# A shorter fallback path behind the last branch: four loops in place of six

## The chip, the core and the metric

The kernel runs on one core of one Trainium2 chip. The core has a matrix engine (PE, with PEld for its weight loads), a vector engine (DVE), a scalar engine (ACT), a general engine (POOL) and SP, which only issues transfers and waits. Each has its own stream of instructions, which is loaded from memory while it runs; in the profile these loads are packets of kind "instruction" (queue q8 for PE, q14 for the others). The metric is the device time of one execution in microseconds; the median of the runs counts.

## What is computed

Pooled attention, then a multiplicative feed-forward block. In the reference, cut to what matters:

```python
# q, k, v: (8, 8, 1152, 64); w1, w2: (512, 1024); w3: (1024, 1024); w_out: (1024, 512)
q_pool = q.reshape(B, H, S // 2, 2, D).mean(axis=3)          # 576 queries
scores = (1 / np.sqrt(D)) * np.matmul(q_pool, k.transpose(0, 1, 3, 2))
scores = scores - np.max(scores, axis=-1, keepdims=True)
attn = np.exp(scores)
attn = attn / (np.sum(attn, axis=-1, keepdims=True) + 1e-09)
x = np.matmul(attn, v)             # then (8 * 576, 512)
out = ((x @ w1) * (x @ w2)) @ w3 @ w_out
```

## The kernel before

The kernel has two paths that compute the same thing. The fast path is one long unrolled program: 32 pairs of heads, scores of 512 columns at a time (L450), exp without the maximum on ACT (L455), the product with the values (L481), and the feed-forward block in chunks of 512 rows filled in between (L590, L628), with w3 and w_out multiplied beforehand into T16. The order on PE is planned when the program is built (`_visits`).

Leaving the maximum out is sound only while the sums of the exponentials stay in a range. The fast path keeps the reciprocal of each sum in `rzall`; near the end DVE compares them with two bounds, a matmul counts how many are inside, and `badi` holds the number of those that aren't. `nc.values_load` reads it into a register of each engine (L1019). At L1022 stands the branch, `tc.If(bad > 0)`: each engine compares its register with zero; if nothing is bad, it jumps over the fallback path, `_general`, to the end of the program. With the inputs of the reference nothing is bad, so `_general` is never executed. It is there, in the instruction streams, between the branch and the end.

The last two chunks of rows (`late_chunks`, L684) run in an order written out by hand (`LATE_ORDER`), in a form with seven products in place of eight (L725), whose sums DVE takes (L776) and whose scaled copies ACT makes (L770, L792). Each finished quarter is stored (`stored`, L736; the transfer itself is L602). `LATE_BY_ACT` names six of these stores that ACT issues on its own transfer queue, q10, in place of SP (q1):

```python
eng = nc.scalar if f"o{k[1]}{k[2]}{c}" in LATE_BY_ACT else nc.sync
...
LATE_BY_ACT = "o00c21 o01c12 o10c12 o10c21 o11c12 o11c21".split()
```

The last of all, o01c12, is ACT's. At the target of the branch (booked under L1022) each engine waits for its own work to be done, and SP for the eight stores that may still be under way, one semaphore after the other; ACT's last four stores stand first, in the order in which they were issued. Behind it, under L1049, SP does twelve further waits that clear the semaphores, and all engines meet at a barrier, twice; there the span ends.

`_general` itself has the loops over batches (`ib`), pairs of heads (`ip`), steps of 96 queries (`iq`, once for each head of a pair, written out twice), tiles of the hidden width (`ift`), and steps of 96 rows for the last product (`iq` again): six in the program. Each loop brings, on every engine, blocks for its entry, its reset with barriers, its back branch and its exit. In the compiled program the instructions between the branch and its target number 261 on PE, 233 on SP, 221 on DVE, 160 on ACT and 156 on POOL, branch labels not counted.

Of the kernel before, what the change touches and what calls it, by code (L numbers as in the profile page):

```python
# [8 lines left out]
FP32 = mybir.dt.float32  # L9
FP16 = mybir.dt.float16  # L10
AF = mybir.ActivationFunctionType
ALU = mybir.AluOpType
# [11 lines left out]
def _general(tc, q, k, v, out, w1sb, w2sb, T16):  # L24

    nc = tc.nc
    B, H, S, D = q.shape
    Sq = S // 2
    NJ = S // 128
    dm = H * D  # L30
    dff = w1sb.shape[2]
    NC = dm // 128
    NF = dff // 128
    QP = 96
    QC = Sq // QP
    SCALE = 0.5 * float(D) ** -0.5
    SCL = 16.0
    W = 384
    kf, qf, vf = (t.rearrange("b h s d -> (b h) s d") for t in (k, q, v))
    with tc.tile_pool(name="gen", bufs=1) as sb, \  # L40
         tc.tile_pool(name="gen_ps", bufs=1, space=bass.MemoryType.PSUM) as ps, \
         tc.For_i(0, B, 1) as ib:
        xT = sb.tile([128, NC * Sq], FP16)
        with tc.For_i(0, H // 2, 1) as ip:
            for u in range(2):
                ih = ib * H + ip * 2 + u
                hs = u * 64
                kst = sb.tile([128, NJ, D], FP32, tag="g_kst")
                nc.sync.dma_start(out=kst, in_=kf[bass.ds(ih, 1)].rearrange("o (c p) d -> p (o c) d", p=128))
                vst = sb.tile([128, NJ, D], FP32, tag="g_vst")  # L50
                nc.sync.dma_start(out=vst, in_=vf[bass.ds(ih, 1)].rearrange("o (c p) d -> p (o c) d", p=128))
                qst = sb.tile([QP, QC, 2, D], FP32, tag="g_qst")
                nc.sync.dma_start(out=qst, in_=qf[bass.ds(ih, 1)].rearrange("o (c p t) d -> p (o c) t d", p=QP, t=2))
                kh = sb.tile([128, NJ, 128], FP16, tag="g_kh")
                qh = sb.tile([QP, QC, 128], FP16, tag="g_qh")
                vh = sb.tile([128, NJ, D], FP16, tag="g_vh")
                nc.vector.memset(kh, 0.0)
                nc.vector.memset(qh, 0.0)
                nc.vector.tensor_copy(out=kh[:, :, 0:D], in_=kst)
                nc.vector.tensor_tensor(out=qh[:, :, 0:D], in0=qst[:, :, 0, :], in1=qst[:, :, 1, :], op=ALU.add)  # L60
                nc.vector.tensor_copy(out=vh, in_=vst)
                kT = sb.tile([128, NJ, 128], FP16, tag="g_kT")
                nc.sync.dma_start(out=kT, in_=kh.rearrange("p c d -> p (c d)"), transpose=True)
                qT = sb.tile([128, QC * QP], FP16, tag="g_qT")
                nc.sync.dma_start(out=qT.rearrange("p (c i) -> p c i", i=QP), in_=qh.rearrange("p c d -> p (c d)"),
                                  transpose=True)
                kTf = kT.rearrange("p c i -> p (c i)")
                with tc.For_i(0, Sq, QP) as iq:
                    qc = sb.tile([128, QP], FP16, tag="g_qc")
                    nc.vector.tensor_copy(out=qc, in_=qT[:, bass.ds(iq, QP)])  # L70
                    pss = ps.tile([128, S // W, 512], FP32, tag="g_pss")
                    for w in range(S // W):
                        nc.tensor.matmul(pss[0:QP, w, 0:W], qc, kTf[:, w * W:w * W + W], start=True, stop=True)
                    mx = sb.tile([QP, 1], FP32, tag="g_mx")
                    nc.vector.tensor_reduce(out=mx, in_=pss[0:QP, :, 0:W], axis=mybir.AxisListType.XY, op=ALU.max)
                    nb = sb.tile([QP, 1], FP32, tag="g_nb")
                    nc.vector.tensor_scalar_mul(out=nb, in0=mx, scalar1=-SCALE)
                    e = sb.tile([QP, S // W, W], FP32, tag="g_e")
                    nc.scalar.activation(out=e, in_=pss[0:QP, :, 0:W], func=AF.Exp, bias=nb, scale=SCALE)
                    z = sb.tile([QP, 1], FP32, tag="g_z")  # L80
                    nc.vector.tensor_reduce(out=z, in_=e, axis=mybir.AxisListType.XY, op=ALU.add)
                    nc.vector.tensor_scalar(out=z, in0=z, scalar1=1e-9, scalar2=None, op0=ALU.add)
                    rz = sb.tile([QP, 1], FP32, tag="g_rz")
                    nc.vector.reciprocal(out=rz, in_=z)
                    eh = sb.tile([QP, S], FP16, tag="g_eh")
                    nc.vector.tensor_scalar(out=eh, in0=e.rearrange("p w i -> p (w i)"), scalar1=rz, scalar2=SCL,
                                            op0=ALU.mult, op1=ALU.mult)
                    eT = sb.tile([128, NJ, QP], FP16, tag="g_eT")
                    nc.sync.dma_start(out=eT, in_=eh, transpose=True)
                    pav = ps.tile([128, 512], FP32, tag="g_pav")  # L90
                    pc = pav[hs:hs + 64, 0:QP]
                    for jt in range(NJ):
                        nc.tensor.matmul(pc, vh[:, jt, :], eT[:, jt, :], start=(jt == 0), stop=(jt == NJ - 1))
                    nc.vector.tensor_copy(out=xT[hs:hs + 64, bass.ds(ip * Sq + iq, QP)], in_=pc)
        gT = sb.tile([128, NF * Sq], FP16)
        NH = Sq // 2
        with tc.For_i(0, NF, 1) as ift:
            for n0 in (0, NH):
                pa = ps.tile([128, 512], FP32, tag="g_pa")
                pb = ps.tile([128, 512], FP32, tag="g_pb")  # L100
                for pw, wt, tg in ((pa, w1sb, "g_w1"), (pb, w2sb, "g_w2")):
                    wc = sb.tile([128, NC, 128], FP16, tag=tg, name=tg)
                    nc.vector.tensor_copy(out=wc, in_=wt[:, :, bass.ds(ift * 128, 128)])
                    for mc in range(NC):
                        nc.tensor.matmul(pw[:, 0:NH], wc[:, mc, :], xT[:, mc * Sq + n0:mc * Sq + n0 + NH],
                                         start=(mc == 0), stop=(mc == NC - 1))
                asb = sb.tile([128, NH], FP32, tag="g_asb")
                nc.vector.tensor_copy(out=asb, in_=pa[:, 0:NH])
                nc.vector.tensor_tensor(out=gT[:, bass.ds(ift * Sq + n0, NH)], in0=pb[:, 0:NH], in1=asb, op=ALU.mult)
        gTv = gT.rearrange("p (f i) -> p f i", i=Sq)  # L110
        with tc.For_i(0, Sq, QP) as iq:
            gc = sb.tile([128, NF, QP], FP16, tag="g_gc")
            nc.vector.tensor_copy(out=gc, in_=gTv[:, :, bass.ds(iq, QP)])
            po = ps.tile([128, 512], FP32, tag="g_po")
            for ft in range(NF):
                nc.tensor.matmul(po[0:QP, :], gc[:, ft, :], T16[:, ft, :], start=(ft == 0), stop=(ft == NF - 1))
            osb = sb.tile([QP, dm], FP32, tag="g_osb")
            nc.vector.tensor_scalar_mul(out=osb, in0=po[0:QP, :], scalar1=1.0 / (SCL * SCL))
            nc.sync.dma_start(out=out[bass.ds(ib * Sq + iq, QP), :], in_=osb)


class _Plan:
# [150 lines left out]
def kernel(  # L273
# [748 lines left out]
    with tc.If(bad > 0):  # L1022
        _general(tc, q, k, v, out, w1sb, w2sb, T16)
# [30 lines left out]
```

## Time and profile before

| | us |
|---|---|
| median of 3 runs | 413.35 |
| lowest and highest run | 413.25, 414.69 |
| the profiled execution | 414.17 |
| its span, first to last instruction | 412.4 |
| last computation ends (DVE, L776) | 404.66 |

A row of the listing by line names a line of the kernel, the engine (a q behind it means its sequencer, so PEldq is PE's), the operation, the count and its shortest, middle and longest duration in ns, then the first and last start in us. A row of the DMA view names a queue, how many packets it moved in the window asked for, their megabytes, and the time of these packets as a share of 16 engines in that window; a row that begins with DMA has the window in 40 slices, each digit the busy share in tenths. A row of stretches has the bounds, the length, and for PE, PEld, DVE, ACT and POOL the busy time and, in brackets, the number of instructions, then the granted clock (1.00 throughout here), the DMA share and GB/s.

### The profile page before, as it was taken

The numbers are of one execution on the slowest core, as the hardware profiler recorded it, in microseconds if no ns is written. First come the engines' busy times: TensorE is split into PE (matmuls) and PEld (weight loads), VectorE is DVE, ScalarE is ACT, GpSimd is POOL, SyncE is SP. The second block draws the span as 40 slices with busy tenths as digits, with TensorE's granted clock in tenths as the row PEclk, the third lists the DMA queues.
The fourth block names the chain that finished last, engine by engine and source line by source line (L and its number), as shares of the span: only waits on it lengthen the run. The fifth ranks groups of instructions, "written<-read, shape, count | busy, mean of one in ns | idle before, by whom it ended". The sixth has DMA issues, their size and how long they took to land.

```text
span 412.4 us, 13099 instructions
## 1 busy us (share of the span) xinstructions
PE 394.8 (96%) x5473; PEld 260.3 (63%) x5473; DVE 218.7 (53%) x594; ACT 335.2 (81%) x380; POOL 212.7 (52%) x237
## 2 busy tenths in 40 slices
PE   3899999999999999999999999999999999999992
PEld 1477887565556655565556555655777655668881
DVE  1255565665356535554455535553655445738971
ACT  4888979898989998899999899999999887037750
POOL 4989976370673316504534355425533995242830
PEclk9999999999999999999999999999999999999998
DMA  8999999999598799939999999997985440030023
GB/s 272 211 330 298 283 296 329 311 239 268 173 264 230 215 264 277 271 56 237 288 282 279 272 265 261 265 302 159 288 226 130 74 102 15 16 114 2 14 76 124
DMA packets 92227, 86.39 MB, mean 209 GB/s; under 512 B 59776, under 2 KB 66176, under 8 KB 92160
## 3 DMA queue, kind: packets, MB, share of 16 engines
q1 hardware_dynamic: 82624, 60.11, 59.7%
q0 software_dynamic: 8384, 24.06, 20.3%
q10 hardware_dynamic: 1152, 1.31, 1.0%
q8 instruction: 44, 0.72, 0.8%
q14 instruction: 23, 0.19, 0.1%
HBM read 67.11 MB, written 9.44 MB: 186 GB/s over the span
## 4 chain that ended last, share of the span: by engine, by line
PE 92%; ACT 2%; DMA 2%; DVE 1%; issue 1%; SPq 0%; POOL 0%; ACTq 0%
PE psc L450 20%; PE avb L481 17%; PE mo L590 15%; PE mo L628 11%; PE mot L590 9%; PE b L725 6%; PE mo L568 3%; PE avb L478 3%; ACT ring L455 2%; PE b L628 2%; PE ptk L390 2%; DMA kst<-in_k_dram 2%; PE mo L725 1%; PE avb L725 1%; DVE kqT L392 1%; PE mot L568 1%
## 5 line engine op out<-in xcount | busy, mean ns | idle before, releaser
L455 ACT ACTIVATE ring<-psc 128x1024 f16<-128x1024 f32 x324 | 308.2, 1025 | 33.5 <-PE psc L450 31.7
L481 PEld LDWEIGHTS <-ring 128*128 128x128 f16 x2304 | 84.4, 98 | 26.3 <-issue 7.1
L450 PE MATMUL psc<-kqT 64*128 64x512 f16 (+7 forms) x1152 | 96.1, 290 | 3.6 <-ACT ring L455 0.9
L481 PE MATMUL avb<-vaug,ring 128*128 128x65 f16 x2304 | 91.4, 193 | 0.0
L362 POOL CAST kq<-kst 128x1152 f16<-128x1152 f32 x31 | 35.7, 1150 | 76.5 <-DMA kqT<-kq 48.7
L450 PEld LDWEIGHTS <-kqT 64*128 64x128 f16 x1152 | 45.9, 95 | 31.0 <-issue 8.3
L628 PE MATMUL mo<-T,gT 128*128 128x512 f16 x192 | 45.6, 380 | 0.0
L502 DVE RECIPROCAL rzall<-avb 128x2 f32<-128x2 f32 x144 | 23.8, 165 | 37.0 <-PE avb L481 20.2
L637 DVE TENSOR_SCALAR osb<-mo 128x512 f32<-128x512 f32 x24 | 16.6, 691 | 48.6 <-PE mo L628 48.6
L366 POOL TENSOR_TENSOR kq<-qst 128x512 f16<-128x512 f32 x31 | 39.4, 1271 | 2.1 <-DMA qst<-in_q_dram 2.1
L375 POOL CAST vaug<-vst 128x1152 f16<-128x1152 f32 x32 | 36.6, 1143 | 6.5 <-DMA vst<-in_v_dram 6.5
L602 POOL DMA_DIRECT2D out_dram<-osb x18 | 9.9, 552 | 54.6 <-DVE rzall L502 54.6
L621 DVE TENSOR_TENSOR gT<-mo,asb 128x512 f16<-128x512 f32 x36 | 24.9, 691 | 24.7 <-PE mo L590 24.3
L590 PE MATMUL mo<-xT,w2sb 128*128 128x512 f16 (+2 forms) x168 | 37.2, 350 | 0.0
L628 PEld LDWEIGHTS <-gT 128*128 128x128 f16 x224 | 19.8, 98 | 25.6 <-issue 5.2
L590 PEld LDWEIGHTS <-w2sb 128*128 128x128 f16 x256 | 21.9, 97 | 20.7 <-issue 4.2
L617 DVE COPY asb<-mo 128x512 f32<-128x512 f32 x32 | 22.1, 691 | 24.0 <-PE mo L590 23.7
L590 PEld LDWEIGHTS <-w1sb 128*128 128x128 f16 x256 | 22.0, 98 | 20.3 <-issue 4.1
L590 PE MATMUL mo<-xT,w1sb 128*128 128x512 f16 (+2 forms) x148 | 33.1, 352 | 0.0
L516 DVE TENSOR_TENSOR xb<-avb,rzall 128x128 f16<-128x128 f32 x96 | 28.0, 291 | 3.3
L590 PE MATMUL mot<-xT,w1sb 128*128 128x512 f16 (+1 forms) x104 | 23.6, 354 | 0.1
L590 PE MATMUL mot<-xT,w2sb 128*128 128x512 f16 (+1 forms) x84 | 19.5, 359 | 0.0
(141 smaller groups left out, 429.6 us busy)
## 6 DMA issues: line engine op xcount, KB each, us to landing
vst<-in_v_dram SPq DMA_DIRECT2D x25, 576.0 KB, 5.0
kst<-in_k_dram SPq DMA_DIRECT2D x23, 576.0 KB, 5.7
qst<-in_q_dram SPq DMA_DIRECT2D x23, 512.0 KB, 6.9
kst<-in_k_dram POOLq DMA_DIRECT2D x8, 576.0 KB, 8.9
out_dram<-osb POOLq DMA_DIRECT2D x18, 256.0 KB, 6.1
qst<-in_q_dram POOLq DMA_DIRECT2D x8, 512.0 KB, 9.7
vst<-in_v_dram POOLq DMA_DIRECT2D x7, 576.0 KB, 6.0
w3c<-in_moe_w_dram POOLq DMA_DIRECT2D x4, 512.0 KB, 7.6
```

Source lines behind the costliest of these rows:

```text
L362: nc.gpsimd.tensor_copy(out=kq16[:, 0:NJ].rearrange("p c u d -> p u c d"), in_=kst.rearrange("p u (c d) -> p u c d", d=D))
L366: eng.tensor_tensor(out=kq16[:, NJ:NJ + QM].rearrange("p c u d -> p u c d"), in0=qv[:, :, :, 0], in1=qv[:, :, :, 1], op=ALU.add)
L375: nc.gpsimd.tensor_copy(out=va[:, :, :, 0:D], in_=vs.pop(p).rearrange("p u (c d) -> p u c d", d=D))
L450: nc.tensor.matmul(psc[:, u, f - s * G:f - s * G + ln], kT2[u * 64:u * 64 + 64, jt, :], qpT[u * 64:u * 64 + 64, i0:i0 + ln], start=True, s ...
L455: nc.scalar.activation(out=ring[:, :, r0:r0 + G], in_=psc, func=AF.Exp, bias=0.0, scale=SCALE)
L481: nc.tensor.matmul(avb[:, o + u * E1:o + u * E1 + E1], ring[:, u, c0:c0 + 128], va[:, u, jt, :], start=(jt == 0 and u == 0), stop=(jt == N ...
L502: nc.vector.reciprocal(out=rzall[:, i, :], in_=av[:, :, D:E1].rearrange("p u o -> p (u o)"))
L516: nc.vector.tensor_tensor(out=xbt, in0=av[:, :, 0:D], in1=rzall[:, i, :].unsqueeze(2).to_broadcast([128, 2, D]), op=ALU.mult)
L590: nc.tensor.matmul(pw[:, d0:d0 + n], wt[:, mc, ft * 128:ft * 128 + 128], xT[:, mc, a:a + n], start=(mc == 0 and d0 == 0), stop=(mc == NC - ...
L621: nc.vector.tensor_tensor(out=t["g"][:, ft, :], in0=pb, in1=t["a"], op=ALU.mult)
L628: nc.tensor.matmul(po, t["g"][:, ft, tt:tt + 128], T16[:, ft, :], start=(ft == 0), stop=(ft == NF - 1))
L725: nc.tensor.matmul(pt[:, n * f:n * f + n], l[:, i, :], b[:, i, :], start=(p in (1, 5) and f == 0 and i == 0), stop=(i == kc - 1), skip_gro ...
```

## The change

Only `_general` is rewritten; the fast path, the check, the branch and the end stay as they are. The loops become `ib`, `iq` (96 queries), `ip` and `ift`: a step takes 96 queries of one batch through everything, attention, both projections, and the last product, so `xT` and `gT` hold 96 columns in place of 576, and K and V are loaded and turned again in each step. The product with T16 and the store stand in the body of `iq` without a loop of their own. Loads, clearing and casts move from SP's queue and DVE to POOL; four small scalings and copies move from DVE to ACT.

The diff, cut to its core:

```diff
-QC = Sq // QP
-         tc.For_i(0, B, 1) as ib:
-        xT = sb.tile([128, NC * Sq], FP16)
+         tc.For_i(0, B, 1) as ib, tc.For_i(0, Sq, QP) as iq:
+        xT = sb.tile([128, NC * QP], FP16)
+        gT = sb.tile([128, NF * QP], FP16)
         with tc.For_i(0, H // 2, 1) as ip:
+            pav = ps.tile([128, 512], FP32, tag="g_pav")
             for u in range(2):
...
-                nc.sync.dma_start(out=kst, in_=kf[bass.ds(ih, 1)]...)
+                nc.gpsimd.dma_start(out=kst, in_=kf[bass.ds(ih, 1)]...)
...
-                qst = sb.tile([QP, QC, 2, D], FP32, tag="g_qst")
+                qst = sb.tile([QP, 2, D], FP32, tag="g_qst")
...
-                nc.vector.memset(kh, 0.0)
-                nc.vector.memset(qh, 0.0)
-                nc.vector.tensor_copy(out=kh[:, :, 0:D], in_=kst)
+                nc.gpsimd.memset(kh, 0.0)
+                nc.gpsimd.memset(qh, 0.0)
+                nc.gpsimd.tensor_copy(out=kh[:, :, 0:D], in_=kst)
...
-                with tc.For_i(0, Sq, QP) as iq:
-                    qc = sb.tile([128, QP], FP16, tag="g_qc")
-                    nc.vector.tensor_copy(out=qc, in_=qT[:, bass.ds(iq, QP)])
-                    pss = ps.tile([128, S // W, 512], FP32, tag="g_pss")
+                pss = ps.tile([128, S // W, 512], FP32, tag="g_pss")
...
-                    nc.vector.tensor_scalar_mul(out=nb, in0=mx, scalar1=-SCALE)
+                nc.scalar.mul(out=nb, in_=mx, mul=-SCALE)
...
-        NH = Sq // 2
         with tc.For_i(0, NF, 1) as ift:
-            for n0 in (0, NH):
...
+                nc.gpsimd.tensor_copy(out=wc, in_=wt[:, :, bass.ds(ift * 128, 128)])
...
+            nc.scalar.copy(out=asb, in_=pw[0][:, 0:QP])
...
-        with tc.For_i(0, Sq, QP) as iq:
-            gc = sb.tile([128, NF, QP], FP16, tag="g_gc")
-            nc.vector.tensor_copy(out=gc, in_=gTv[:, :, bass.ds(iq, QP)])
-            po = ps.tile([128, 512], FP32, tag="g_po")
-            for ft in range(NF):
-                nc.tensor.matmul(po[0:QP, :], gc[:, ft, :], T16[:, ft, :], ...)
+        po = ps.tile([128, 512], FP32, tag="g_po")
+        for ft in range(NF):
+            nc.tensor.matmul(po[0:QP, :], gT[:, ft * QP:ft * QP + QP], T16[:, ft, :], ...)
...
-            nc.vector.tensor_scalar_mul(out=osb, in0=po[0:QP, :], scalar1=1.0 / (SCL * SCL))
+        nc.scalar.mul(out=osb, in_=po[0:QP, :], mul=1.0 / (SCL * SCL))
```

The matmuls written in the new path are, per pair of heads, 2 x (3 + 9), per tile of the hidden width 2 x 4, and 8 for the last product. By the change's own words the branch spans 134 to 212 instructions, depending on the engine, in place of 181 to 286, branch labels counted.

## The prediction

> **What bounds the kernel now.** I read the page first, for the whole span.
>
> ```profile
> span 412.4 us, 13099 instructions
> PE 394.8 (96%) x5473; PEld 260.3 (63%) x5473; DVE 218.7 (53%) x594; ACT 335.2 (81%) x380; POOL 212.7 (52%) x237
> q8 instruction: 44, 0.72, 0.8%
> q14 instruction: 23, 0.19, 0.1%
> ```
>
> TensorE sets the pace for 404 us, and the change touches no instruction that runs in them: it rewrites the code that the last branch skips. So only the end counts. The last two rows are code being loaded: 44 packets of 16 KB for PE (0.72 MB; 10,946 matmuls and weight loads, so one packet holds about 250 instructions), and 8 KB packets, about 125 instructions, for the others. Next the chain of waits from 403 us on, and the instructions that the listing by line gives for the branch, L1022.
>
> ```profile
> 404.24 0.42 DVE room L776
> ...
> L1022 POOLq COMPARE_BRANCH  x1: 45/45/45, 394.6 to 394.6; - x1
> L1022 PEldq COMPARE_BRANCH  x1: 4046/4046/4046, 402.2 to 402.2; - x1
> L1022 SPq COMPARE_BRANCH  x1: 58/58/58, 403.3 to 403.3; - x1
> L1022 DVEq COMPARE_BRANCH  x1: 72/72/72, 404.2 to 404.2; - x1
> L1022 PEldq EVENT_SEMAPHORE  x1: 51/51/51, 406.3 to 406.3; - x1
> L1022 ACTq COMPARE_BRANCH  x1: 54/54/54, 406.6 to 406.6; - x1
> L1022 ACTq EVENT_SEMAPHORE  x1: 17/17/17, 407.0 to 407.0; - x1
> L1022 DVEq EVENT_SEMAPHORE  x1: 21/21/21, 407.3 to 407.3; - x1
> ```
>
> The last computation ends at 404.66, the span at 412.39: 7.7 us are stores, branch and closing barrier. ACT is through its branch in 0.4 us (406.6 to 407.0). PE needs 4.1 (402.2 to 406.3), DVE 2.6 after its last operation (404.66 to 407.3). These two went for code that wasn't there. Nobody waits for them, though: the barrier comes at 411.5. SP decides, which waits at L1022 for eight stores, then does twelve waits of L1049. Four narrow windows of these two lines (407.5 to 408, 409.9 to 410.1, 410 to 411, 410.9 to 411.5) give its times:
>
> ```profile
> L1022 SPq EVENT_SEMAPHORE  x2: 17/17/17, 407.6 to 407.8; - x2
> L1022 SPq EVENT_SEMAPHORE  x2: 17/17/17, 410.0 to 410.1; - x2
> L1049 SPq EVENT_SEMAPHORE  x8: 27/28/28, 410.3 to 410.8; - x8
> L1049 SPq EVENT_SEMAPHORE  x4: 28/28/28, 411.2 to 411.4; - x4
> ```
>
> Between 407.85 and 409.98 SP waits for one store, ACT's last. After it there are 2.4 us of waits 0.07 apart, with one hole of 0.41 (410.8 to 411.2). What keeps that store is in the DMA view, for the windows 406.9 to 408.6, 407 to 407.2, 407.5 to 408.5 and 408.6 to 409.9:
>
> ```profile
> q10 hardware_dynamic: 177, 0.15, 25.9%
> q14 instruction: 3, 0.02, 6.1%
> ...
> q8 instruction: 1, 0.02, 56.4%
> DMA  1202910100000090000000000000000000000000
> DMA  0000002001001002000200100000000000000000
> q10 hardware_dynamic: 9, 0.01, 3.8%
> ```
>
> q10 is ACT's queue. Its packets run on all engines until 407.7 (third DMA row, the single 1 in its eighth slice), then nothing for a microsecond, then nine packets one behind the other, 408.8 to 409.5. A store has 128 rows, eight for each of 16 DMA engines: the nine are one engine's share. It was held by code: a PE block that began at 407.0 and took 1.80 us (56.4% of 16 engines over 0.2 us) and three 8 KB blocks. The PE block is the one after PE's branch target, fetched as PE resumed at 406.3.
>
> An earlier block does the same to ACT's issues. Its DMAs of L602 before and after 403.7, and the block at 403.2 (window 403.1 to 403.3: 51.4% of 16 engines over 0.2 us, 1.64 us):
>
> ```profile
> L602 ACTq DMA_DIRECT2D out_dram<-room x3: 339/350/357, 398.1 to 403.3; - x3
> L602 ACTq DMA_DIRECT2D out_dram<-room x3: 388/700/1428, 403.8 to 406.1; - x3
> q8 instruction: 1, 0.02, 51.4%
> ```
>
> The last three lose 1428 - 350 + 700 - 350 = 1.43 us while that block is ahead of the stores.
>
> **The change, part by part.** First the spans. The compiled program of before skips 261 instructions on PE, 221 on DVE, 233 on SP, 160 on ACT, 156 on POOL (the title's 181 to 286 count 25 labels more). Of this, one loop costs an idle engine 24 to 26 instructions. With four loops that fixed part is 104; PE adds 2 x 12 + 8 + 8 matmuls with their weight loads, 80, and about 10 waits: 195. DVE adds 13 operations, five register steps, some waits: 128. SP, which counts more semaphores in each loop: about 160. POOL, with loads, casts and memsets that are new to it: 130; ACT 117.
>
> Where the branches stand in their blocks follows from the last fetch ahead of each: code packets in the windows 389.6 to 389.8 (PE) and 349 to 349.2 (DVE). POOL's branch at 394.6 and its packet at 395.7 (window 394.7 to 396.5, slice 23 of 40) say to set these back by 1 us.
>
> ```profile
> q8 instruction: 1, 0.02, 27.4%
> q14 instruction: 1, 0.01, 11.3%
> DMA  0000000000000000000000400000000000000000
> 388.60:402.20 13.60, 13.60 (x127) 12.19 (x126) 10.91 (x20) 7.75 (x21) 6.42 (x6) 1.00 0.24 71
> 348.00:404.30 56.30, 56.20 (x584) 43.96 (x582) 41.44 (x85) 25.53 (x54) 22.87 (x19) 1.00 0.17 53
> ```
>
> PE has taken 253 instructions since its block began, a whole block: with 261 more it leaves the current and the next block (514 of 500), with 195 (448) it stays inside. DVE has 85 operations, about 100 with its waits: 321 of 250 before, 228 after. So both targets come inside what is loaded. ACT's and POOL's were inside and stay. SP's position can't be read closely enough; 160 or 233 give the same block or both a new one, so I take it as unchanged.
>
> Now the terms, against this execution's 414.17 us (span 412.39 and 1.78 around it).
>
> 1. PE's and DVE's own stalls, 3.6 and 2.5 us over ACT's 0.4: worth nothing, the 411.5 barrier hides them. Without that cover PE's would be the whole 3.6.
>
> 2. The fetches. A hit still brings the next block about 1 us after the branch (POOL's row), so PE's block at 403.2 remains, and DVE's at 405.3 (first row below, window 405.2 to 405.4). The second ones, after resuming, go: PE's at 407.0 and one 8 KB block. The held share then ends with the others. Their last packet is at 407.7; the held one's last, 409.45, was seen by SP at 409.98, 0.53 later; so SP sees the store at 408.2 instead of 409.98: -1.78. Bounds: SP's wait before it is at 407.85, so at most -2.1; if two 8 KB blocks, 0.4 us each by 6.1% of 16 engines over 1.7 us for three (0.55 each at most), still stand ahead, the share ends about 1.3 later: -0.5.
>
> ```profile
> q14 instruction: 1, 0.01, 19.2%
> q14 instruction: 1, 0.01, 6.4%
> ```
>
> 3. The hole of 0.41 among SP's 0.07-steps is like ACT's and POOL's 0.4 on passing into another block, and a code packet follows it (second row, window 412 to 412.3). SP's shorter span moves its last 25 instructions some 70 earlier, off that border: -0.34; bounds 0 and -0.34.
>
> 4. ACT's issues: the block at 403.2 stays, so 0. Bound: -1.4, if it goes or comes later.
>
> 5. More POOL work, nb, asb and osb on ACT, the smaller tiles: only in the skipped code, 0. Nothing ahead of the branch is moved. No row can show an added wait there; the bound is the spread of the three runs, 1.4 us (413.25 to 414.69).
>
> Sum -1.78 - 0.34 = -2.12: this execution 412.05, and on the median of the runs, 413.35, which stands 0.82 below it, 411.2 us.
>
> The Trainium skill, page "Runtime: NRT & Kernel Launch", section "Instruction fetch mechanics", says that a taken branch out of the two loaded pages stalls for a fetch; the stalls above agree. It gives pages of 16 KiB for every engine and 2048 instructions of room on PE; by that no target here, 156 to 261 instructions off, was missing before, and the time would stay 413.35, as in the first rival below. The 8 KB packets and PE's 4.1 us branch speak against those sizes.
>
> **The rivals.** *Nothing moves.* No target was missing: the window is wider than two packets and PE's 4.1 us is something that any branch behind a deep queue pays; or PE's position is off by more than the 50 instructions that I leave (500 - 448). Then both PE blocks stay. For it: my positions come from packet times. Against: DVE, with a short queue, shows 2.6 and two blocks. DVE's and the hole alone: 413.0 to 413.35.
>
> *More goes.* PE's block at 403.2 was the missing target itself; if a hit fetches nothing until PE runs on, ACT's three issues follow at 0.35 each, DVE's last result (404.66) becomes the bound, and the last store starts 1.4 earlier: 411.2 - 1.4 = 409.8. Against: POOL's hit did bring a block.
>
> *Slower: a hit becomes a miss.* ACT branches last, at 406.6. If its new target falls out of what is loaded, it pays PE's 4.1, and behind PE's block 1.8 more: 406.6 + 5.9 = 412.5, past the barrier at 411.5, so the end moves by 0.9: 414.3. It decides once ACT comes back after 411.5, so a price over 4.9. Against: its branch hit with 160 instructions and now has 117.
>
> **How the numbers follow.** The forecast gets 0.52, more goes 0.22, nothing moves 0.16, slower 0.10. Half a per cent, 2.07 us, about what a measurement of this kernel can tell from no change, puts the bound for faster at 411.28: the forecast lies on it. Term 2 is bounded unevenly but term 4 can only add, so I put 0.34 of the 0.52 beyond it and 0.18 within. Faster 0.34 + 0.22 = 0.56; same 0.18 + 0.16 + 0.05 = 0.39; slower 0.05, the half of its case that the runs' spread lifts from 414.3 over 415.4. The forecast's own range is 410.9 to 412.85 (2.44 to 0.5 off the median). The range runs from all terms at their far bounds (413.35 - 2.1 - 0.34 - 1.4 = 409.5) to just over no change, 413.5.
>
> **What would show it.** Right: PE's branch under 0.1 us, PE and DVE at L1022 some 0.4 us after branching; one 16 KB block after 402, none near 407; no lone packets behind the store; SP's third and fourth waits at L1022 within 0.4 us; no hole at L1049; ACT's L602 still with a 1.4 us issue. Wrong: PE's branch still at 4 us; a second PE block; a last store as late as 410 with no code ahead of it; ACT resuming late.

## The result, and the profile after

Over 22 runs each, taken in turn, the changed kernel has a median of 411.76 us beside 414.44 before; the ratio is 0.9946 with a 95% interval of 0.9923 to 0.9969, 2.2 us (1.3 to 3.2) of 414. (The ratio goes by the fast runs alone; the two medians, of all runs, are 2.7 us apart, which lies inside the interval.) On the 413.35 of the runs shown ahead of the prediction that makes 411.1. The profiled execution took 411.33.

The page, and the last row of DVE's timeline:

```profile
span 409.7 us, 13103 instructions
q8 instruction: 43, 0.70, 0.7%
q14 instruction: 21, 0.17, 0.1%
...
404.23 0.42 DVE L764 SCALAR_TENSOR_TENSOR room<-b,room 128x256 f32<-128x256 f32 x1
```

The last computation ends at 404.65, as before (404.66). All of the 2.7 us lie behind it. I call the time from this end to the end of the span the tail: 412.4 - 404.66 = 7.7 before, 409.7 - 404.65 = 5.0 after. One 16 KB block and two 8 KB blocks fewer were loaded. The branch now stands at L1010; its instructions by line:

```profile
L1010 POOLq INC_SWDGE_SEM  x1: 1411/1411/1411, 396.1 to 396.1; - x1
L1010 PEldq COMPARE_BRANCH  x1: 358/358/358, 402.2 to 402.2; - x1
L1010 SPq COMPARE_BRANCH  x1: 58/58/58, 403.3 to 403.3; - x1
L1010 PEldq EVENT_SEMAPHORE  x1: 51/51/51, 404.2 to 404.2; - x1
L1010 DVEq COMPARE_BRANCH  x1: 72/72/72, 404.2 to 404.2; - x1
L1010 DVEq EVENT_SEMAPHORE  x1: 21/21/21, 404.8 to 404.8; - x1
L1010 ACTq COMPARE_BRANCH  x1: 54/54/54, 405.7 to 405.7; - x1
L1010 ACTq EVENT_SEMAPHORE  x1: 17/17/17, 406.2 to 406.2; - x1
```

PE's branch takes 0.36 us in place of 4.05 (its next row waits for its own last matmul), and DVE is back 0.2 us after its last operation in place of 2.6. POOL has a new 1.4 us step, over 12 us ahead of the end. SP's waits, by three narrow windows of L1010 (406.9 to 407.7, 407.7 to 408.02) and L1037, the end of the program (408 to 408.75):

```profile
L1010 SPq EVENT_SEMAPHORE  x3: 17/17/17, 407.0 to 407.7; - x3
L1010 SPq EVENT_SEMAPHORE  x4: 17/17/17, 407.7 to 408.0; - x4
L1037 SPq EVENT_SEMAPHORE  x12: 27/28/28, 408.0 to 408.7; - x12
```

The two microseconds between the third and the fourth wait are gone, and so is the hole among the twelve. And the first list has seven waits, not eight: the one for ACT's last store, told by the semaphore numbers in the trace, is missing there and is only met as the eighth of the second list. ACT's last three issues (L590), the PE block in the window 403.7 to 404, and code and store packets in 406.5 to 407.2, then 407.2 to 409.5:

```profile
L590 ACTq DMA_DIRECT2D out_dram<-room x3: 368/387/936, 403.8 to 405.3; - x3
q8 instruction: 1, 0.02, 18.8%
...
q14 instruction: 2, 0.02, 13.4%
DMA  0100100000000000000000000000000000000000
q10 hardware_dynamic: 11, 0.01, 1.2%
```

The only PE block comes with the branch and takes 0.90 us (18.8% of 16 engines over 0.3 us; before, 1.64). Near 407 there are two 8 KB blocks and no 16 KB block, and the last store's packets are through by 407.6; before, the last of them came at 409.5. ACT's three issues take 1.69 us, 0.83 less than before.

### The profile page after: what moved, and what is told of

Read it like the earlier page. It is cut to its first block, busy times and chain, and to the rows that moved or that the text cites. A ratio compares the mean times of both kernels' runs of the same rounds, so it can differ in the third digit from the quotient of the medians.

```text
span 409.7 us, 13103 instructions
## 1 busy us (share of the span) xinstructions
PE 394.7 (96%) x5473; PEld 260.2 (64%) x5473; DVE 218.6 (53%) x594; ACT 335.2 (82%) x380; POOL 213.0 (52%) x237
## 4 chain that ended last, share of the span: by engine, by line
PE 93%; ACT 2%; DVE 2%; DMA 1%; issue 1%; ACTq 0%
PE psc L438 20%; PE avb L469 17%; PE mo L578 15%; PE mo L616 11%; PE mot L578 9%; PE b L713 7%; PE mo L556 3%; PE avb L466 3%; ACT ring L443 2%; PE b L616 2%; PE ptk L378 2%; PE mo L713 1%; DMA qst<-in_q_dram 1%; PE avb L713 1%; DVE kqT L380 1%; PE mot L556 1%
## 5 line engine op out<-in xcount | busy, mean ns | idle before, releaser
L590 POOL DMA_DIRECT2D out_dram<-osb x18 | 9.9, 552 | 54.1 <-DVE rzall L490 54.1
```

## The experiments

The comparisons go by the tail of one profile each, since the time ahead of it moves by more than 1 us from run to run whatever the kernel (the last computation ended between 404.1 and 406.4); the tail of the unchanged new kernel was 5.0 and 4.8 in two profiles; of the kernel before there is one. Spans are given to 0.1 us, so a tail is good to 0.1. The ratio is that of the times to the kernel before, with its interval.

| kernel | last result, span | tail | ACT's last three issues | ratio |
|---|---|---|---|---|
| before | 404.66, 412.4 | 7.7 | 2.52 | 1 |
| after | 404.65, 409.7 | 5.0 | 1.69 | 0.9946 (0.9923 to 0.9969) |
| after again | 404.38, 409.2 | 4.8 | 2.18 | 0.9950 (0.9937 to 0.9964) |
| PE long | 404.09, 410.1 | 6.0 | 2.16 | 0.9980 (0.9962 to 0.9998) |
| before, PE short | 404.54, 410.7 | 6.2 | 2.50 | 0.9975 (0.9954 to 0.9995) |
| eighth semaphore | 404.92, 410.3 | 5.4 | 2.16 | 0.9948 (0.9926 to 0.9969) |
| SP long | 405.99, 412.1 | 6.1 | 2.13 | 0.9984 (0.9954 to 1.0015) |
| DVE long | 404.12, 409.3 | 5.2 | 2.48 | 0.9945 (0.9929 to 0.9961) |
| PE shifted | 404.87, 409.7 | 4.8 | 1.20 | 0.9942 (0.9917 to 0.9966) |
| SP shifted | 404.64, 409.9 | 5.3 | 2.40 | 0.9938 (0.9916 to 0.9961) |
| both shifted | 404.98, 409.8 | 4.8 | 1.23 | 0.9944 (0.9929 to 0.9960) |
| no fallback | 406.39, 409.6 | 3.2 | 1.17 | 0.9917 (0.9893 to 0.9940) |

**PE's span alone, both ways.** In the new kernel, PE made long again; in the kernel before, PE made short:

```diff
-        for ft in range(NF):
+        for ft in [*range(NF)] * 5:
             nc.tensor.matmul(po[0:QP, :], gT[:, ft * QP:ft * QP + QP], T16[:, ft, :], ...)
```

> The new kernel with the last product of the fallback written five times over, so that PE's branch spans 259 instructions again and no other engine's changes; the fallback isn't executed. Theory (PE's missed block holds the last store): PE's branch takes about 4 us again, a second 16 KB block stands near 407.0, ACT's last three issues take 1.4, 0.7 and 0.4 us, the last store lands near 410 and SP, which in the new kernel waits for it only in its second list, is stopped there: span about 411.2, 1.5 over the new kernel's 409.7. Rival (the gain is SP's order of waits and the border that its target no longer meets): PE's branch may be slow but the span stays at 409.7.

```diff
-                    for jt in range(NJ):
+                    for jt in range(2):
...
-                    for mc in range(NC):
+                    for mc in range(1):
...
-            for ft in range(NF):
+            for ft in range(1):
```

> The kernel of before, whose fallback leaves out 33 of its matmuls (two of nine value products per head, one of four steps of each projection, one of eight of the last product are left), so that PE's branch spans 195 in place of 261 and no other engine's changes. Theory: PE's branch under 0.4 us, no 16 KB block near 407, ACT's issues about 0.8 us shorter in all, the last store seen at about 408.1 in place of 410.0, the hole of 0.4 between SP's waits still there: span about 410.5 in place of 412.4. Rival (order of waits, border): span 412.3 to 412.4.

PE long: the branch and the return, code packets in 406 to 407.4, and SP's second list behind 408:

```profile
L1010 PEldq COMPARE_BRANCH  x1: 3762/3762/3762, 401.7 to 401.7; - x1
L1010 PEldq EVENT_SEMAPHORE  x1: 51/51/51, 405.5 to 405.5; - x1
...
q8 instruction: 1, 0.02, 7.2%
...
L1037 SPq EVENT_SEMAPHORE  x5: 28/28/28, 408.9 to 409.1; - x5
```

The missed branch, the second 16 KB block and the wait are back: five of the twelve waits, the one for the last store first among them, come only from 408.9 on. The tail is 6.0, 1.0 to 1.2 over the new kernel, not 1.5: with the wait that late in SP's lists, part of the store's delay is covered by other waits. PE short, with its branch, the third and fourth wait (407.6 to 408.3) and the second list (408.55 to 409.2, 409.4 to 409.75):

```profile
L1022 PEldq COMPARE_BRANCH  x1: 358/358/358, 402.1 to 402.1; - x1
...
L1022 SPq EVENT_SEMAPHORE  x2: 17/17/17, 407.7 to 408.2; - x2
...
L1049 SPq EVENT_SEMAPHORE  x8: 27/28/28, 408.6 to 409.1; - x8
L1049 SPq EVENT_SEMAPHORE  x4: 28/28/28, 409.5 to 409.7; - x4
```

With PE's span alone, the third and the fourth wait are 0.5 apart in place of 2.1, and the hole is still there. The tail falls by some 1.5 us. The expected 0.8 on ACT's issues did not come: they take 2.50, as before.

**SP's first list, and the hole.** The fallback's load of K on SP's queue, once and then twelve times:

```diff
-                nc.gpsimd.dma_start(out=kst, in_=kf[bass.ds(ih, 1)]...)
+                nc.sync.dma_start(out=kst, in_=kf[bass.ds(ih, 1)]...)
```

> The new kernel with the fallback's load of K on SP's queue in place of POOL's, so that its SP transfers use all eight semaphores again and the wait for the last store goes back into SP's first list, as before the change. Theory: the store is there at about 408.1, so SP is held 0.35 us longer than its other waits need: span 410.1, 0.4 over the new kernel. Rival (the order of waits is the main gain): span near 411.8, 2 us over.

```diff
-                nc.gpsimd.dma_start(out=kst, in_=kf[bass.ds(ih, 1)]...)
+                for _ in range(12):
+                    nc.sync.dma_start(out=kst, in_=kf[bass.ds(ih, 1)]...)
```

> The kernel with the eighth semaphore (K loaded on SP's queue in the fallback) with that load written twelve times, so that SP's branch spans 232 instructions, as before the change (233), in place of 186. Theory: the hole of 0.41 us among SP's waits in its second list is back, after about the eighth of them, and the tail is 0.35 longer than with the load written once (5.4). Rival (the hole was a wait for another engine): no hole.

With the load once, the third and the fourth wait of the first list:

```profile
L1010 SPq EVENT_SEMAPHORE  x2: 17/17/17, 408.0 to 408.3; - x2
```

With the load twelve times, the first three waits, the next five, and the second list:

```profile
L1011 SPq EVENT_SEMAPHORE  x3: 17/17/17, 408.4 to 409.0; - x3
L1011 SPq EVENT_SEMAPHORE  x5: 17/17/17, 410.0 to 410.3; - x5
L1038 SPq EVENT_SEMAPHORE  x12: 27/28/28, 410.4 to 411.1; - x12
```

Once: the fourth wait stands 0.37 behind the third (407.96 and 408.33), and the tail is 5.4, 0.4 to 0.6 over the new kernel: the expected 0.4. So the seven transfers that the new fallback has on SP's queue save this much, since SP's first list waits only for the semaphores that the fallback uses. Twelve times: there is a hole, but not at the eighth wait of the second list. It stands 13 places earlier, ahead of the fourth wait of the first list, which is now 1.0 behind the third, and costs 0.7 of tail. One packet of q14 follows it, as it did before. The twelve loads make ten more machine instructions than my count of SP's span shows, which accounts for most of the shift; the other three places are open. The ratio, 1.5 us over that with the load once, isn't explained by a tail 0.7 longer; the intervals are wide enough to overlap (0.9954 to 1.0015 and 0.9926 to 0.9969), and it stays open whether the rest is real.

**DVE's span alone.**

```diff
+        pad = sb.tile([QP, 1], FP32, tag="g_pad")
+        for _ in range(95):
+            nc.vector.memset(pad, 0.0)
         osb = sb.tile([QP, dm], FP32, tag="g_osb")
```

> The new kernel with 95 memsets of a spare tile in the fallback, so that DVE's branch spans 224 instructions again. Theory: DVE resumes 2.6 us after its last result in place of 0.2, a further 8 KB block follows some 0.65 us later, near 408, and the end moves by 0 to 0.3 us since nobody waits for DVE. Rival (any missed branch costs its full stall): 2.4 us.

DVE's rows, and code in the window 407.2 to 407.5:

```profile
L1013 DVEq COMPARE_BRANCH  x1: 72/72/72, 403.7 to 403.7; - x1
L1013 DVEq EVENT_SEMAPHORE  x1: 21/21/21, 406.7 to 406.7; - x1
...
q14 instruction: 1, 0.01, 12.8%
```

DVE is late by 2.6 us (404.12 to 406.7), its second block comes at 407.3, and the tail is 5.2: 0.2 to 0.4 longer, hardly more than the 0.2 between the two profiles of the unchanged kernel. The ratio doesn't move. So this missed branch costs at most a fraction of what it lasts.

**Is ACT's shorter issue part of the change?** The unchanged new kernel, a second time:

> The new kernel once more, unchanged, for a second profile: ACT's last three issues took 0.37, 0.94 and 0.39 us in its first profile, with PE's block at 403.9, but 1.4, 0.4 and 0.4 and 1.3, 0.8 and 0.4 in the two experiments with the same PE span and the block at 403.1 to 403.5. If the block follows the branch by 1 us as a rule and the first profile was an exception, the issues take some 2.1 us in all, as before the change (2.5), and the tail is 5.0 to 5.4; if the first profile is the rule, they take 1.7.

```profile
L590 ACTq DMA_DIRECT2D out_dram<-room x3: 399/632/1150, 403.5 to 405.3; - x3
...
q8 instruction: 1, 0.02, 94.7%
```

(The packet begins at 402.74, 0.65 us after PE's branch began; it takes 1.5 us.) The first profile, where this block came 1.7 us after the branch, was the exception. Issues of 2.1 to 2.2 us are the rule for the new kernel, 0.3 to 0.4 less than before. In the table, the three kernels whose DVE misses have 2.48 to 2.52, with PE's span short or long; the new kernel with DVE's span long is one of them. So the 0.3 to 0.4 seem to go with DVE's hit and not with PE's, though SP shifted, where DVE hits, has 2.40. One profile of each doesn't prove it.

**No code at all, and code at another time.** Branch and fallback left out:

```diff
-    with tc.If(bad > 0):
-        _general(tc, q, k, v, out, w1sb, w2sb, T16)
```

> The new kernel without branch and fallback: the check of the sums is computed and read, but nothing hangs on it. No 8 KB block is fetched for a branch; PE may still bring one 16 KB block, since its stream ends at a border. Theory: ACT's last three issues take 0.35 us each if no PE block comes at 403 to 404, the last store is issued by 405.1 and there by 407.2, and the end follows SP's list: span 408.3 to 408.8. Rival (the stores themselves need this long, code or not): span 409.7.

```profile
L590 ACTq DMA_DIRECT2D out_dram<-room x4: 338/378/408, 405.1 to 406.5; - x4
...
SPq L1035 <- DMA out_dram<-room: 2.6, 3, 2.0
```

No block is fetched for a branch, ACT's issues take 0.34 to 0.41 each, SP's longest wait for a store is one transfer long, and the tail is 3.2. So 4.5 of the 7.7 us of before, and 1.6 to 1.8 of what is left, belong to a path that never runs. Not all of this is code on the way: without the branch only four waits stand behind the one for the last store, and the end comes 1.2 us after it, where the new kernel's end comes 2.0 us after SP's third wait. The span, 409.6, is outside the expected 408.3 to 408.8, because this execution reached its last result 1.7 us later than the new kernel's first profile; the tail itself is shorter than the 3.6 to 4.2 that this range stood for. The rival's 409.7 fits it only by that; the tail and the ratio of 0.9917 decide against it.

Then the blocks were moved instead. PE: 20 tiny matmuls in its idle first 5 us, so that its border passes 40 instructions ahead of the branch. SP: 16 transfers of 4 bytes behind its first loads.

```diff
+    for _ in range(20):
+        nc.tensor.matmul(avb[0:1, 0:1], ident16[:, 0:1], ident16[:, 0:1], start=True, stop=True)
...
+    spare = const.tile([1, 16], FP32)
+    for i in range(16):
+        nc.sync.dma_start(out=spare[0:1, i:i + 1], in_=q[0, 0, 0:1, i:i + 1])
```

> The new kernel with 20 tiny matmuls more on PE at the start, while PE waits for its first loads (until 5.0 us), so that all of PE's later instructions stand 40 places further on in the 16 KB blocks: PE passes the border some 40 instructions ahead of its branch and the target, 195 on, lies in the same block. Theory: no PE block is fetched at the branch; the one for the border comes some 2 us earlier, near 401 to 402; ACT's last three issues take 0.35 to 0.4 us each and the last store is issued 0.5 after DVE's last result, so the tail after that result shrinks from 5.0 to about 4.4: median 0.6 to 1 us below the new kernel's. Rival (ACT's issues are slow for another reason, such as SP's stores under way): issues as before, no change.

> The new kernel with 16 transfers of 4 bytes into a spare tile behind SP's first loads, where SP has nothing to issue for some 50 us: 14 instructions more on SP, so that SP passes its border that many instructions ahead of the branch and its target, 174 on, lies in the block that is then loaded. Theory: SP comes out of its branch in 0.4 to 0.6 us in place of 3.6, one 8 KB block near 2.2 to 2.6 us after the last result is gone; PE's block at the branch stays and still holds ACT's issues and the stores, so the tail shrinks from 4.8 to 5.0 only to 4.6 to 4.9. Rival (SP's own miss sets the end): the tail shrinks by 0.8 or more.

> Both shifts, PE's 20 matmuls and SP's 16 small transfers. Theory (in the run with PE's shift alone SP's own missing block took the place of PE's: SP was back at 2.36, a store lay ready from 1.34, and 8 KB blocks from 1.2 to 2.5 held the third store until 2.84): now nothing holds the stores, the third is there by 2.1 to 2.3, the fourth by 2.5, and SP's list after it takes 1.9: tail 4.1 to 4.3, 0.7 below the new kernel, ratio to before near 0.992. Rival (the rest is the stores' own time and the list): tail 4.8 to 5.0.

PE shifted: ACT's issues, the PE block (401.5 to 401.7), SP's branch and its first three waits (407.1 to 407.8):

```profile
L590 ACTq DMA_DIRECT2D out_dram<-room x3: 391/402/412, 404.0 to 405.0; - x3
q8 instruction: 1, 0.02, 37.3%
L1012 SPq COMPARE_BRANCH  x1: 58/58/58, 404.0 to 404.0; - x1
L1012 SPq EVENT_SEMAPHORE  x3: 17/17/17, 407.2 to 407.7; - x3
```

The mechanism did as expected: the PE block came 0.9 us ahead of the branch, and ACT's last issue began at 405.0, 0.15 after DVE's last result. The block fell on an issue of SP's instead, which took 1.13 us. But the tail stayed at 4.8. SP came back only at 407.2, 3.2 us after its branch, though the first store that it waits for, issued at 403.55, had landed 2.7 us later: its own target was missing. That isn't what set the end, though. SP's third wait, for ACT's last store but one, ended as that store landed, at 407.7, 2.9 us after the last result; the end came 2.0 us later, as it did in the first and the second profile of the new kernel and in those with DVE long, SP shifted and both shifted.

With SP's shift alone PE's block still held ACT's issues (2.40) and the tail was 5.3, longer than expected; why stays open. With both, SP was through its first wait by 406.3, but its third ended at 407.8, again 2.9 us after the last result: SP's missing target had cost PE shifted nothing. SP's first three waits (406.2 to 407.9), its issues and the code packets among the stores:

```profile
L1015 SPq EVENT_SEMAPHORE  x3: 17/17/17, 406.3 to 407.8; - x3
...
L590 SPq DMA_DIRECT2D out_dram<-room x6: 338/395/870, 400.7 to 403.8; - x6
...
q14 instruction: 3, 0.02, 7.5%
```

The PE block now stood among SP's issues (870 ns in place of 0.4 us for one of them), and three 8 KB blocks (406.1 to 407.6) came while the stores were under way: tail 4.8. That these blocks are what now holds the last store but one is likely, but no run moved them alone. The expected 4.1 to 4.3 was wrong, and none of the three is told from the new kernel by its ratio. I ran no version that is clearly better than both with the fallback in place.

## Why the prediction was right

*The forecast time.* 411.2 stood against 411.1, and the range held it. The 0.54% lies on the 0.5% bound, as was said.

*Term 1, the stalls themselves are worth nothing.* Right: making DVE miss again returned its 2.6 us stall and 0.2 to 0.4 of tail at most.

*Term 2, the store held by second blocks, -1.78.* The mechanism was right and the size somewhat high. PE's span alone gave some 1.5 of tail in the kernel before, 1.0 in the ratio (0.2 to 1.9), and 1.0 to 1.2 in the new kernel; DVE's block adds 0.4 at most. I let the held share end with the others; with PE short the store was still seen 0.5 after the third wait, probably because of the two 8 KB blocks near 407.6. The bound of -0.5 doesn't follow from its own figures: two blocks of 0.4 to 0.55 make 0.8 to 1.1, not 1.3, which leaves -1.0 to -0.7.

*Term 3, the hole, -0.34.* Right as a border of SP's stream: it stays with PE short, goes with SP's shorter span, and returns at another place with SP long.

*Term 4, ACT's issues, 0.* Nearly right. The first profile seemed to say -0.8, which the second one didn't bear out; 0.3 to 0.4 is left. One reading under it was wrong: the block at 403.2 was over by 404.85 (1.64 us), while the 700 ns issue of before began at 405.34; beside that stood an 8 KB block, the one of 405.28. That PE's block after a hit comes about 1 us after the branch was nearly right: in seven profiles in which PE's target lay in the next block it came 0.65 to 1.02 us after the branch, but for the first, with 1.7.

*Not in the sum.* SP's first list lost the wait for the last store, worth 0.4 to 0.6 by the tails and 0.37 by the wait itself. It came from the loads that moved to POOL, a part that I costed at 0 because it is only in skipped code; but what the skipped code uses decides for which semaphores the jumping path waits. Term 2 was a little too large and this was missing. The measured parts (1.5, at most 0.4, 0.34 and 0.4 to 0.6) add to some 2.2 to 2.8, beside a tail shorter by 2.7 to 2.9 and a ratio worth 2.2 (1.3 to 3.2). The sum of 2.12 meets the ratio and falls short of the tail, so that it met the median so closely is partly luck.

*The counts.* PE 195 and ACT 117 were exact, DVE has 130 for 128, SP 174 for 160; POOL has 171 where I had 130, and came back 1.2 us after its branch (394.6 to 395.8), far ahead of the end.

*The signs.* Most were as named. Two weren't: PE's branch takes 0.24 to 0.36 us on a hit, not under 0.1, and ACT's longest issue took 0.94 and 1.15 us in the two profiles, not 1.4.

*The rivals.* "Nothing moves" and the block sizes that go with it fell: 64 instructions more on PE make the branch miss again. "More goes" fell with the second profile: a hit fetches the next block soon after the branch; only when the border was moved ahead of the branch did ACT issue at 0.4. "Slower" did not come about: ACT was back in 0.5 us.

## What to carry to other kernels

Code that is never executed can cost time at the end of a kernel: look at each engine's branch row and at the instruction packets in the stretch where the last stores are under way. Count how far each target lies from its branch, and ask not how long an engine waits for its code but which data packets stand behind it. After such a block is moved away, look for the wait that now ends last before counting the gain: here SP's missing target looked like the limit, and a store was.

## What the runs showed of the hardware that was not expected

- The loading of code and the stores share DMA engines: a 16 KB block takes 0.9 to 1.8 us and holds one engine's sixteenth of each store behind it, though the other fifteen are done.
- A transfer queue feels it at its issue: beside a PE block a DMA issue took 0.94 to 1.43 us on ACT and up to 1.13 on SP, where ACT's take 0.34 to 0.41 without code.
- A hit isn't free either: ACT came out of its branch 0.4 to 0.5 us later in every run, and PE's brought another block 0.65 to 1.7 us after the branch. In straight code, passing a border cost SP 0.34 us (a step of 0.41 among steps of 0.07), and 0.65 in the run with SP long, counted from the landing of the store that it waited for.
